# Second layer of an FNet block: the first of seven Strassen products taken in two levels too, in a unit of three

## The chip, the cores and the metric

One core of one Trainium2 chip. The metric is the device time of one execution in microseconds (us). The kernel before takes 1074.35 us, the median of three runs (1073.09 to 1074.63). The engines are called PE (TensorE, matmul), DVE (VectorE), ACT (ScalarE), POOL (GpSimd) and SP (SyncE, which issues most DMA transfers here).

## The reference

Eight batches, 576 tokens, 8 heads of 64, all in fp32. Linear attention is followed by an FNet block with width D = 512 and a two-layer network of 2048 hidden values:

```python
q_s = softmax(q, axis=-1); k_s = softmax(k, axis=2)
kv = einsum('bhsd,bhse->bhde', k_s, v)
x = einsum('bhsd,bhde->bhse', q_s, kv)           # -> (B, S, 512)
mixed = real(fft(fft(x, axis=1), axis=2))
u = x + mixed
un = (u - mean(u)) / sqrt(var(u) + 1e-06)
out = u + maximum(un @ w_ch1, 0.0) @ w_ch2       # 512 -> 2048 -> 512
```

## The kernel before, in words

*Tiling.* The 8 × 576 tokens are nine groups of 512. The first group goes through the two layers with plain matmuls while the weights are prepared. The other eight are called order 1 to order 8 (in code, `order` up to `B` = 8). Each order has an `up` stage (first layer, 512 → 2048) and a `down` stage (second layer, 2048 → 512, added to `u`). Meanwhile the attention and the Fourier mix of the next group are interleaved, so that each order finds its normalised input `unT` ready.

*One level.* A layer is a matrix product A·B cut into 2 × 2 blocks, computed by the Strassen–Winograd scheme with seven products of half size, numbered 1 to 7 and taken in `ORDER` = (1, 6, 5, 7, 2, 4, 3). Each product has its own left side (a sum of blocks of A, slots 0 to 6) and right side (a sum of blocks of B). The left sides of the second layer are the hidden activations, made in `up`: four blocks come out of the first layer, and `a_side` (L383 to L386) makes four sums of blocks of 128 × 512 for each of four pairs j. `A_AT` tells which slot a product reads.

*Two levels.* In orders 2 to 8, `deep_down` computes most of the seven products of the second layer by seven inner products again. Two of them, a unit such as (2, 4), run interleaved: for each inner number n of `ORDER` one inner product of each. An inner product is four matmuls of 128 columns in the source, which the trace holds as eight records on PE; its right side, 128 × 512, is one of the blocks of `w2d` in DRAM. `a_step` (L1317) makes the inner left sides: number 4, 5, 2 and 6 are sums of two 128 × 512 blocks in SBUF. The three PSUM banks `ba`, `bb`, `bc` collect the inner products (`place`), and `ends` empties them: a copy `s1` and the copy `out(0)` on ACT, and on DVE `plus` (L1378): `u2` = bb + s1 after n = 6, `u3` = bb + s1 and `out(3)` after n = 7, `out(2)` after n = 4 and `out(1)` after n = 3, which closes the unit. Product n = 7 adds into the same bank `bb` that `u2` reads. With the unit closed, its two results lie in SBUF, and `into` (L1321, a sum of 128 × 512) adds each to a quarter of the group's output; `sums` (L1324) adds one result to another. Both run on `E`: POOL in orders 2 to 7 and DVE in order 8.

Orders 2 to 7 take product 1 in one level (`single`, L1341: 16 source matmuls of 256 columns, 32 records), then the units (2, 4), (7, 6), (5, 3). Order 8 takes singles 1 and 2, the units (7, 6) and (5, 3), and single 4. Order 1 takes all seven in one level; during it `deepen` (L1279) makes the inner right sides of products 2 to 7, two subtractions on DVE and two on POOL for each, and SP stores the blocks to `w2d` (L1285), 42 blocks of 256 KB.

*Weights.* They stream from DRAM through four slots of 1 MB. `plan` lists the pieces in the order of their use (eight of the first layer an order, then those of the second); when PE has issued the last matmul of piece n, `used` has SP load piece n + 4 into its slot (L454).

*What sets the order.* Each step carries a written-out time, in units of 0.87 us from order 1 on: PE's inner product takes one unit, a stage `up` 56 (`UP`), a stage `down` 50 (`TWICE`) in orders 2 to 8. The steps are sorted by that time and issued, and each engine runs its instructions in this order; it waits by semaphores for what an instruction needs. During `down` the mix of the next group runs: five `block` products (L997, L1000), then two sets of `mix` steps, three in orders 2, 4 and 6. A set of mix steps copies on ACT, computes `eo` from a PSUM bank on DVE (L1042, L1043), and adds it to the rows of `x` (L1054 for 257 columns, L1055 for 255, both SBUF to SBUF on DVE). `norm` for the next group follows at 29 units; in order 7 it is at 14.

Of the kernel before, what the change touches and what calls it, by code (L numbers as in the profile page):

```python
# [78 lines left out]
UNITS = ((2, 4), (7, 6), (5, 3))  # L79
DEEP = [(m, n) for unit in UNITS for n in ORDER for m in unit]  # L80
UP, TWICE = NP * len(ORDER), 8 + 6 * len(ORDER)
# [55 lines left out]
class _Block:  # L137
    def __init__(self, ctx, tc, q, kT, v, w1, w2, ft, cd, out):
# [51 lines left out]
        self.plan, self.base = [], {}  # L190
        for at in range(1, B + 1):
            self.base[at] = len(self.plan)
            self.plan += [self.w1s[p][:].rearrange("p a n -> p (a n)") for pair in PAIRS for p in pair]
            one = lambda m: self.w2s[WB_AT[m]].rearrange("p a n -> p (a n)")
            first = self.first_deep(at)
            self.plan += [one(m) for m in (ORDER if at == 1 else (1, 2) if at == B else (1,))]
            if at > 1:
                for i in range(first, len(DEEP), 4):
                    self.plan.append(self.w2d[:, i:min(i + 4, len(DEEP)), :].rearrange("p a n -> p (a n)"))
            if at == B:  # L200
                self.plan.append(one(4))
# [242 lines left out]
    def first_deep(self, order):  # L444

        return 2 * len(ORDER) * (order == B)

    def load(self, n):

        if n >= len(self.plan):  # L450
            return
        k = (n + 3) % 4
        w = self.big[:, k * NP * HD:(k + 1) * NP * HD]
        self.nc.sync.dma_start(w[:, :self.plan[n].shape[1]], self.plan[n])  # L454
        self.stream[n] = w.rearrange("p (a n) -> p a n", n=HD)
# [776 lines left out]
    def up(self, order, g):  # L1232

        nc, V = self.nc, self.nc.vector
        steps = []
        base, e = self.base[order], V if order == B else nc.gpsimd
        for j in range(NP // 2):
            hp = lambda i, h=self.hpairs(j, 2): h[:, :, i, :]

            def product(m, bank, first, j=j):  # L1240
                def run(i):
                    w = self.stream[base + 2 * j + i]
                    for k in range(2):
                        nc.tensor.matmul(bank()[:, i, :], lhsT=w[:, WA_AT[m], k * P:(k + 1) * P],  # L1244
                                         rhs=self.unT[g][:, B_AT[m], k, :], start=first and i == 0 and k == 0,
                                         stop=k == 1,
                                         skip_group_check=True)
                return [lambda i=i: run(i) for i in range(2)]

            def c11(bank, _, hp=hp):  # L1250
                return [(0, lambda: nc.scalar.activation(hp(0), bank()[:], ACT.Relu))]

            def other(i, hp=hp):
                def run(bank, u):
                    steps = [(0, lambda: V.tensor_tensor(out=hp(i), in0=bank()[:], in1=u()[:], op=ALU.add)),  # L1255
                             (0.8, lambda: nc.scalar.activation(hp(i), hp(i), ACT.Relu))]  # L1256
                    if i == 2:
                        steps.append((1.6, lambda: self.a_side(hp, hp, e, e)))
                    return steps
                return run  # L1260

            job = self.strassen(product, 1, {(1, 1): c11, (2, 1): other(1), (2, 2): other(3), (1, 2): other(2)})
            t = 2 * len(ORDER) * j
            steps += at(t, job) + [(t + 2 * len(ORDER) - 0.5 + 5 * i * (j < NP // 2 - 1), lambda n=base + 2 * j + i: self.used(n)) for i in range(2)]
        return steps
# [25 lines left out]
    def deep_down(self, g, order):  # L1291

        nc, V, G = self.nc, self.nc.vector, self.nc.gpsimd
        base, last, skip = self.base[order] + NP, order == B, self.first_deep(order)
        E = V if last else G
        order = (1, 2, *UNITS[1:], 4) if last else (1, *UNITS)
        h = [self.hpairs(p) for p in range(NP)]
        un = lambda i: self.unT[g][:, i].rearrange("p k n -> p (k n)").rearrange("p (f n) -> p f n", n=P)
        dead = lambda m: lambda i: self.hblock(A_AT[m], *((0, 1), (1, 0), (1, 1))[i])
        temps = {4: lambda i: un(i), 2: lambda i: un(3 + i), 7: self.gap, 6: dead(1), 5: (lambda i: un(i)) if last else dead(4), 3: (lambda i: un(3 + i)) if last else dead(2)}  # L1300
        result = {m: self.hblock(A_AT[m], 0, 0) for m in A_AT}
# [6 lines left out]
        def own(m):  # L1308
            def get(i):
                return temps[m](i - 4) if i > 3 else self.hblock(A_AT[m], i // 2, i % 2)  # L1310
            return get

        def a_step(m, o):
            x, y, e, op = {4: (2, 3, V, ALU.add), 5: (4, 0, V, ALU.subtract), 2: (0, 2, V, ALU.subtract),
                           6: (1, 5, E, ALU.subtract)}[o]
            to = own(m)
            e.tensor_tensor(out=to(o), in0=to(x), in1=to(y), op=op)  # L1317
# [12 lines left out]
        def bank(n, size=P):  # L1330
            box[n] = self.ps.tile([P, 2, size], F32, tag=n, name=n)

        def temp(n):
            box[n] = self.work.tile([P, 2, P], F32, tag=n, name=n, bufs=1)
            return box[n][:]

        def single(m, n, name, i, q):
            if q == 0 and (m != 1 or i == 0):
                bank(name, HD)
            for p in range(4 * q, 4 * q + 4):  # L1340
                nc.tensor.matmul(box[name][:, i, :], lhsT=h[p][:, A_AT[m], i * P:(i + 1) * P],  # L1341
                                 rhs=self.stream[n][:, p, :], start=p == 0 and (m != 1 or i == 0), stop=p == NP - 1,
                                 skip_group_check=True)
            if (i, q) == (1, 1):
                self.used(n)

        def one():
            nc.scalar.copy(tile(1), box["bb"][:].rearrange("p c (e n) -> p c e n", n=P))
# [10 lines left out]

        def product(unit, n, i):  # L1360
            m = unit[i]
            q = DEEP.index((m, n))
            q -= skip
            chunk = base + 1 + last + q // 4
            w = self.stream[chunk]
            first = i == 0 and n in (1, 6, 5)
            if first:
                bank(place[n])
            for f in range(4):
                r = q % 4 * 4 + f  # L1370
                nc.tensor.matmul(box[place[n]][:, i, :], lhsT=own(m)(A_AT[n])[:, f, :],  # L1371
                                 rhs=w[:, r // 2, r % 2 * P:r % 2 * P + P], start=first and f == 0, stop=f == 3,
                                 skip_group_check=True)
            if q % 4 == 3 or q + skip == len(DEEP) - 1:
                self.used(chunk)
# [4 lines left out]
        def ends(unit, n):  # L1380
            first, last = (A_AT[m] for m in unit)
            step = last - first
            out = lambda j: self.hpairs(j)[:, first:last + (1 if step > 0 else -1):step, 0:P]
            if n == 1:
                nc.scalar.copy(temp("s1"), box["ba"][:])
            if n == 6:
                plus(temp("u2"), "bb", "s1")
            if n == 7:
                plus(temp("u3"), "bb", "s1")
# [3 lines left out]
            if n == 4:  # L1393
                plus(out(2), "bb", "s1")
# [3 lines left out]
        after = {(2, 4): [(7, into, 1, 0, 4), (9, into, 0, 0, 2)],  # L1398
# [3 lines left out]
        names = {1: ("bb", "bb"), 2: ("bc", "bb"), 4: ("ba", "bb")}  # L1402
        n, t = 2 * len(ORDER), 0
        for i, unit in enumerate(order):
            if unit in A_AT:
                w = base + (i if i < 2 else 2 + (len(DEEP) - skip) // 4)
                for k in range(4):
                    put(t + 2 * k, single, unit, w, names[unit][k // 2], k // 2, k % 2)
                t += 8
                if unit == 1:  # L1410
                    put(t - 0.5, one)
                    put(t + 1, into, 0, 0, 1)
                    continue
                for c in range(2):
                    put(t - 4.5 + 4 * c, add, names[unit][c], unit // 4, 0, c)
                    if unit == 4 and c == 0:
                        steps.extend(self.scatter(t - 3.7, g, c, 1, lambda: self.xpart(g, 0, 1)))
                    else:
                        half(t - 3.7 + 4 * c, c, unit // 4, 0)
                continue  # L1420
            step = 3 if i < 3 else 2
            early = 6 if last and t < n + 8 else 0 if t == 8 else t - n + 2 if i == 2 else t - n + (0 if last else 3)
            for k, o in enumerate((4, 5, 2, 6)):
                for j, m in enumerate(unit):
                    put(early + step * k + j * 1.1 + 0.3, a_step, m, o)
            for k, o in enumerate(ORDER):
                for j in range(2):
                    put(t + 2 * k + j, product, unit, o, j)
                put(t + 2 * k + 1.5, ends, unit, o)
# [3 lines left out]
        if last:  # L1433
            half(t - 8 + 2, 1, 1, 1)
# [7 lines left out]
    def down(self, g, order):  # L1442
# [5 lines left out]
        for k, m in enumerate(ORDER):  # L1448
            if m != 1:
                spare = [self.hblock(A_AT[ORDER[k - 1]], a, b) for a in range(2) for b in range(2)]  # L1450
                n = self.base[order] + NP + k
                steps += at(t * k - 4 * (k % 2 == 0), self.deepen(m, n, spare if k % 2 else [self.gap(i) for i in range(4)]))

        def product(m, bank, first):
            n = self.base[order] + NP + ORDER.index(m)

            def run(i, q):
                w = self.stream[n]
                for p in range(4 * q, 4 * q + 4):
                    nc.tensor.matmul(bank()[:, i, :], lhsT=h[p][:, A_AT[m], i * P:(i + 1) * P], rhs=w[:, p, :],  # L1460
# [74 lines left out]
def kernel(ctx: ExitStack, tc: tile.TileContext, q, kT, v, w1, w2, ft,  # L1535
# [3 lines left out]
    def timed(t, order, g):  # L1539
# [4 lines left out]
        if b == B:  # L1544
            return steps + at(t + UP + 14, blk.norm(groups[b]))
# [139 lines left out]
```

## Time and profile before

| what | value |
|---|---|
| median of three runs | 1074.35 us (1073.09 to 1074.63) |
| profiled execution, its own time | 1072.76 us |
| span of that execution, mean granted clock | 1071.0 us, 0.999 |
| PE busy | 1058.3 us (99%), 6394 records |
| DVE busy | 685.9 us (64%), 1317 instructions |
| POOL busy | 422.5 us (39%), 352 instructions |
| ACT busy | 404.8 us (38%), 953 instructions |
| DMA | 235.9 MB, mean 220 GB/s; SP's queue busy 63.8% of 16 engines' span |
| `down` of order 2 from / 3 / 4 / 5 | 358.1 / 474.9 / 589.6 / 706.5 us |
| `down` of order 6 / 7 / 8 from | 821.2 / 924.5 / 1021.2 us |
| last matmul, end of the span | 1066.7, 1071.0 us |

The span runs from the first to the last instruction that the profiler recorded; the execution's own time has what lies around it, 1.8 us more. The records of PE's matmuls overlap, so the distance between two starts tells what one costs, not its duration. A line number in a view is that of the code printed above, of the kernel before; the lines of the changed kernel lie 15 to 20 further down.

### The profile page before, as it was taken

To read this page: it belongs to the slowest core of one execution; us is meant where nothing else is said; L and a number is where in the kernel's file an instruction comes from. 1 tells how busy PE (TensorE), PEld (TensorE's weight loads), DVE (VectorE), ACT (ScalarE), POOL (GpSimd) and SP (SyncE) were. 2 spreads that over 40 slices of the span, in tenths; PEclk is the share of its full clock that TensorE was granted. 3 is DMA by queue.
4 is the path that set the end of the run, shared out by engine and by line. 5 is a ranking of instruction groups with operands and counts; after the bars stand their busy time and mean duration, and the time that the engine had idled before them with its cause. 6 is when DMAs were issued, how large, how long until landed. Compare 5 with 4: busy or idle time off the path is not lost.

```text
span 1071.0 us, 16992 instructions
## 1 busy us (share of the span) xinstructions
PE 1058.3 (99%) x6394; PEld 922.4 (86%) x6394; DVE 685.9 (64%) x1317; ACT 404.8 (38%) x953; POOL 422.5 (39%) x352
## 2 busy tenths in 40 slices
PE   8999999999999999999999999999999999999998
PEld 7744556988898899889998999889988998899898
DVE  6897787684455874677556765687457742563563
ACT  5675534632245215521453234522552132131210
POOL 3262220265412743454515543374336353552000
PEclk9999999999999999999999999999999999999999
DMA  9486578648976576646755576547644674576464
GB/s 341 160 302 245 174 246 292 208 162 282 329 262 212 179 252 233 225 177 202 273 178 190 196 246 224 199 183 256 222 167 158 210 257 164 203 249 217 176 214 146
DMA packets 112933, 235.90 MB, mean 220 GB/s; under 512 B 22756, under 2 KB 74212, under 8 KB 102228
## 3 DMA queue, kind: packets, MB, share of 16 engines
q1 hardware_dynamic: 112244, 233.90, 63.8%
q8 instruction: 51, 0.84, 0.3%
q10 hardware_dynamic: 480, 0.52, 0.1%
q0 software_dynamic: 128, 0.39, 0.1%
q14 instruction: 30, 0.25, 0.1%
HBM read 199.66 MB, written 38.93 MB: 223 GB/s over the span
## 4 chain that ended last, share of the span: by engine, by line
PE 84%; DVE 3%; ACT 2%; issue 1%; POOL 1%; DMA 0%; POOLq 0%; DVEq 0%; ACTq 0%
PE bb L1244 15%; PE bb L1371 10%; PE bc L1244 10%; PE ba L1244 10%; PE bc L1371 6%; PE ba L1371 6%; PE bb L1341 4%; PE acc L716 2%; PE acc L884 2%; PE bc L1181 2%; PE bb L1460 2%; PE acc L997 2%; PE acc L1000 2%; PE acc L1025 2%; PE bc L1460 1%; PE ba L1460 1%
## 5 line engine op out<-in xcount | busy, mean ns | idle before, releaser
L1244 PE MATMUL bb<-unT,big 128*128 128x256 f32 x768 | 184.4, 380 | 0.8 <-DVE u L1214 0.8
L1244 PEld LDWEIGHTS bb<-unT,big 128*128 128x128 f32 x768 | 142.5, 190 | 20.3 <-DVE u L1214 2.3
L383 POOL TENSOR_TENSOR big<-big 128x512 f32<-128x512 f32 x28 | 35.9, 1281 | 255.9 <-ACT big L1256 255.9
L1256 ACT ACTIVATE big<-big 128x512 f32<-128x512 f32 x96 | 60.6, 631 | 194.9 <-DVE big L1255 194.5
L1244 PE MATMUL ba<-unT,big 128*128 128x256 f32 x512 | 123.8, 379 | 0.0
L1244 PE MATMUL bc<-unT,big 128*128 128x256 f32 x512 | 123.5, 380 | 0.0
L1214 DVE TENSOR_TENSOR u<-bb,s 128x512 f32<-128x512 f32 x66 | 45.6, 691 | 117.7 <-PE bb L1244 97.4
L1371 PE MATMUL bb<-big 128*128 128x128 f32 x848 | 105.2, 275 | 1.8 <-DVE u L1378 1.8
L1244 PEld LDWEIGHTS bc<-unT,big 128*128 128x128 f32 x512 | 94.7, 190 | 12.5 <-DVE big L1255 1.0
L1244 PEld LDWEIGHTS ba<-unT,big 128*128 128x128 f32 x512 | 94.4, 190 | 12.2 <-issue 0.5
L1371 PEld LDWEIGHTS bb<-big 128*128 128x128 f32 x848 | 99.6, 192 | 2.2 <-DVE u L1378 2.2
L1321 POOL TENSOR_TENSOR x<-x,big 128x512 f32<-128x512 f32 x45 | 57.7, 1297 | 62.7 <-issue 32.9
L1317 DVE TENSOR_TENSOR big<-big 128x512 f32<-128x512 f32 x94 | 78.1, 875 | 2.5 <-POOL big L386 2.5
L1371 PE MATMUL ba<-big 128*128 128x128 f32 x640 | 79.6, 275 | 0.0
L766 ACT ACTIVATE q<-q,qm 128x64 f32<-128x64 f32 x248 | 67.5, 342 | 31.2 <-DVE qm L760 25.9
L1371 PEld LDWEIGHTS ba<-big 128*128 128x128 f32 x640 | 76.3, 192 | 1.2
L1341 PE MATMUL bb<-big 128*128 128x256 f32 x256 | 58.7, 380 | 0.0
L1378 DVE TENSOR_TENSOR u<-bb,s 128x256 f32<-128x256 f32 x40 | 16.8, 421 | 64.6 <-PE bb L1371 59.9
L1255 DVE TENSOR_TENSOR big<-bc,u 128x512 f32<-128x512 f32 x64 | 44.0, 687 | 21.9 <-PE bc L1244 21.0
L1341 PEld LDWEIGHTS bb<-big 128*128 128x128 f32 x256 | 48.2, 190 | 8.0 <-DVE big L1255 1.1
L1371 PE MATMUL bc<-big 128*128 128x128 f32 x416 | 51.5, 275 | 0.0
L1371 PEld LDWEIGHTS bc<-big 128*128 128x128 f32 x416 | 48.9, 192 | 0.0
(265 smaller groups left out, 2014.8 us busy)
## 6 DMA issues: line engine op xcount, KB each, us to landing
big<-w2d SPq DMA_DIRECT2D x67, 1024.0 KB, 4.8
big<-w1s SPq DMA_DIRECT2D x64, 896.0 KB, 4.9
big<-w2s SPq DMA_DIRECT2D x16, 1024.0 KB, 6.4
big<-in_w_dram SPq DMA_DIRECT2D x21, 512.0 KB, 6.3
w2d<-big SPq DMA_DIRECT2D x42, 256.0 KB, 5.6
q<-in_q_dram SPq DMA_DIRECT2D x28, 256.0 KB, 6.4
k<-in_kT_dram SPq DMA_DIRECT2D x24, 288.0 KB, 5.6
v<-in_v_dram SPq DMA_DIRECT2D x24, 256.0 KB, 4.4
```

The lines of the kernel that those rows point to most:

```text
L383: e1.tensor_tensor(out=to(4), in0=at(2), in1=at(3), op=ALU.add)
L716: nc.tensor.matmul(pk, lhsT=ks[:, c, :], rhs=v[:, c, :], start=(c == 0), stop=(c == NC - 1))
L766: nc.scalar.activation(q[:, h, :], q[:, h, :], ACT.Exp, bias=m[:, h:h + 1])
L1214: plus = lambda t: V.tensor_tensor(out=temp(t), in0=box["bb"][:], in1=box["s1"][:], op=ALU.add)
L1244: nc.tensor.matmul(bank()[:, i, :], lhsT=w[:, WA_AT[m], k * P:(k + 1) * P], rhs=self.unT[g][:, B_AT[m], k, :], start=first and i == 0 and ...
L1255: steps = [(0, lambda: V.tensor_tensor(out=hp(i), in0=bank()[:], in1=u()[:], op=ALU.add)), (0.8, lambda: nc.scalar.activation(hp(i), hp(i) ...
L1256: (0.8, lambda: nc.scalar.activation(hp(i), hp(i), ACT.Relu))]
L1317: e.tensor_tensor(out=to(o), in0=to(x), in1=to(y), op=op)
L1321: E.tensor_tensor(out=x, in0=x, in1=tile(m), op=ALU.add)
L1341: nc.tensor.matmul(box[name][:, i, :], lhsT=h[p][:, A_AT[m], i * P:(i + 1) * P], rhs=self.stream[n][:, p, :], start=p == 0 and (m != 1 or ...
L1371: nc.tensor.matmul(box[place[n]][:, i, :], lhsT=own(m)(A_AT[n])[:, f, :], rhs=w[:, r // 2, r % 2 * P:r % 2 * P + P], start=first and f == ...
L1460: nc.tensor.matmul(bank()[:, i, :], lhsT=h[p][:, A_AT[m], i * P:(i + 1) * P], rhs=w[:, p, :], start=first and i == 0 and p == 0, stop=p == ...
```

## The change

Product 1 of the second layer joins the first unit of orders 2 to 7, which becomes (1, 2, 4): three outer products run interleaved, with the inner order (1, 5, 6, 2, 7, 4, 3); the other units keep `ORDER`. In that unit n = 4 gets the bank `ba` and is added to `u3` instead of `bb` and `s1`. A down stage of orders 2 to 8 has 49 units of time instead of 50. Along with it:

- `deepen` also runs for product 1 in order 1, so `w2d` has 49 blocks, and is read by 13 pieces an order (the last of one block) instead of one of `w2s` and eleven.
- Slots 2 and 3 of the left sides change places, so that products 1, 2, 4 lie side by side and one instruction of `ends` empties all three. The `a_step`s write their sums to other dead buffers.
- All `a_step`s of the first unit run on DVE (number 6 ran on POOL). Four more of them are there, for product 1. `into` of product 1 comes 5 units after the unit, ahead of the two at 7 and 9; it came just after the single. The ACT copy `one` is gone.
- In `up`, the `a_side` of the last pair j = 3 runs on DVE instead of POOL, and 4.5 units later (2.8 in order 8).
- Order 7: all sums (`E`, and every `a_side`) on DVE; `norm` for the last group at 26.4 units instead of 14.
- Order 8: singles 1 and 2 become a two-level unit (1, 2), its pieces cut from the same blocks with product 4 left out; single 4 stays.

```diff
-UNITS = ((2, 4), (7, 6), (5, 3))
-DEEP = [(m, n) for unit in UNITS for n in ORDER for m in unit]
-UP, TWICE = NP * len(ORDER), 8 + 6 * len(ORDER)
+UNITS = ((1, 2, 4), (7, 6), (5, 3))
+WITHIN = {1: (1, 5, 6, 2, 7, 4, 3), 7: ORDER, 5: ORDER}
+DEEP = [(m, n) for unit in UNITS for n in WITHIN[unit[0]] for m in unit]
+UP, TWICE = NP * len(ORDER), 7 * len(ORDER)
+SLOT = {0: 0, 1: 1, 2: 3, 3: 2, 4: 4, 5: 5, 6: 6}
+H_AT = {m: SLOT[i] for m, i in A_AT.items()}
...
-        base, e = self.base[order], V if order == B else nc.gpsimd
+        base, e = self.base[order], V if order >= B - 1 else nc.gpsimd
+        wait = {1: 0, B: 2.8}.get(order, 4.5)
...
-                        steps.append((1.6, lambda: self.a_side(hp, hp, e, e)))
+                        steps.append((1.6 + wait * (j == NP // 2 - 1), lambda e=V if order > 1 and j == NP // 2 - 1 else e: self.a_side(hp, hp, e, e)))
...
-        E = V if last else G
-        order = (1, 2, *UNITS[1:], 4) if last else (1, *UNITS)
+        E = V if order >= B - 1 else G
+        order = ((1, 2), *UNITS[1:], 4) if last else UNITS
...
-        temps = {4: lambda i: un(i), 2: lambda i: un(3 + i), 7: self.gap, 6: dead(1), 5: (lambda i: un(i)) if last else dead(4), 3: (lambda i: un(3 + i)) if last else dead(2)}
+        temps = {1: self.gap, 2: un, 4: lambda i: un(3 + i), 7: lambda i: self.gap((0, 1, 3)[i]), 6: lambda i: un((0, 1, 6)[i]),
+                 5: (lambda i: un(3 + i)) if last else dead(4), 3: dead(2)}
...
-                           6: (1, 5, E, ALU.subtract)}[o]
+                           6: (1, 5, V if m in UNITS[0] else E, ALU.subtract)}[o]
...
+        def bank_of(unit, n):
+            return "ba" if n == 4 and unit[0] == 1 else place[n]
...
-                plus(out(2), "bb", "s1")
+                plus(out(2), *(("ba", "u3") if unit[0] == 1 else ("bb", "s1")))
...
-        after = {(2, 4): [(7, into, 1, 0, 4), (9, into, 0, 0, 2)],
+        after = {(1, 2, 4): [(5, into, 0, 0, 1), (7, into, 1, 0, 4), (9, into, 0, 0, 2)], (1, 2): [(4, into, 0, 0, 1), (5, into, 0, 0, 2)],
...
-                if unit == 1:
-                    put(t - 0.5, one)
-                    put(t + 1, into, 0, 0, 1)
-                    continue
...
+            size = len(unit)
+            n = size * len(ORDER)
+            if i == 0:
+                starts = (0.2, 2.5, 8.5 if size == 3 else 5.5, 11.5 if size == 3 else 7)
+            else:
+                early, step = (max(t - 11, 7), 3) if i == 1 else (t - 11 - 3 * last, 2)
+                starts = [early + step * k + 0.3 for k in range(4)]
+            for at_o, o in zip(starts, (4, 5, 2, 6)):
                 for j, m in enumerate(unit):
-                    put(early + step * k + j * 1.1 + 0.3, a_step, m, o)
-            for k, o in enumerate(ORDER):
-                for j in range(2):
-                    put(t + 2 * k + j, product, unit, o, j)
-                put(t + 2 * k + 1.5, ends, unit, o)
+                    put(at_o + j * (1.1 if i else 0.75), a_step, m, o)
+            for k, o in enumerate(WITHIN[UNITS[i][0]]):
+                for j in range(size):
+                    put(t + size * k + j, product, unit, o, j)
+                put(t + size * k + size - 0.5, ends, unit, o)
...
-            return steps + at(t + UP + 14, blk.norm(groups[b]))
+            return steps + at(t + UP + 26.4, blk.norm(groups[b]))
```

## The prediction

> **What bounds the kernel now.** First the shares of busy time and the chain of waits. The first line below gives busy time per engine; the second is the chain that ended last, by engine.
>
> ```profile
> PE 1058.3 (99%) x6394; PEld 922.4 (86%) x6394; DVE 685.9 (64%) x1317; ACT 404.8 (38%) x953; POOL 422.5 (39%) x352
> ...
> PE 84%; DVE 3%; ACT 2%; issue 1%; POOL 1%; DMA 0%; POOLq 0%; DVEq 0%; ACTq 0%
> ```
>
> TensorE (PE) sets the time, at a granted clock of 0.999. Its matmul records overlap, so their busy time says little; I use the distance from one start to the next. Summed over the trace, distances beyond the normal come to only some 11 us, most of it in the opening. So a matmul less is time gained, and a wait of PE is time lost in full.
>
> Second, the groups by line, for what the change touches: output and inputs, shape, count, then busy us and mean ns, then idle time before and its releaser.
>
> ```profile
> L1371 PE MATMUL bb<-big 128*128 128x128 f32 x848 | 105.2, 275 | 1.8 <-DVE u L1378 1.8
> ...
> L1341 PE MATMUL bb<-big 128*128 128x256 f32 x256 | 58.7, 380 | 0.0
> ...
> L1317 DVE TENSOR_TENSOR big<-big 128x512 f32<-128x512 f32 x94 | 78.1, 875 | 2.5 <-POOL big L386 2.5
> ```
>
> PE waits within the two-level units for one thing only: the sum `u` that DVE makes (L1378). And L1317, sums of the same size, averages 875 ns where an undisturbed one takes 0.68 us: something holds it up.
>
> Third, the timeline around the end of the first unit of order 4, where PE next depends on DVE (start, duration, engine, line; x2 is two in a row):
>
> ```profile
> 617.48 0.42 DVE L1378 TENSOR_TENSOR big<-bc,u 128x256 f32<-128x256 f32 x1 [0.69 <-PE bc L1371]
> 617.83 0.42 DVE L1054 TENSOR_TENSOR x<-x,eo 128x257 f32<-128x257 f32 x1
> 618.16 1.49 DVE L1055 TENSOR_TENSOR x<-x,eo 128x255 f32<-128x255 f32 x1
> 619.57 0.74 DVE L1042 TENSOR_TENSOR eo<-acc,sn 128x256 f32<-128x256 f32 x2
> ...
> 621.32 0.68 DVE L1317 TENSOR_TENSOR big<-big 128x512 f32<-128x512 f32 x1
> 621.92 0.41 DVE L1378 TENSOR_TENSOR u<-bb,s 128x256 f32<-128x256 f32 x1
> ...
> 618.04 2.74 POOL L1321 TENSOR_TENSOR x<-x,big 128x512 f32<-128x512 f32 x2 [8.79 <-issue]
> ...
> 617.28 1.95 PE L1371 MATMUL ba<-big 128*128 128x128 f32 x16
> ...
> 622.64 1.95 PE L1371 MATMUL bb<-big 128*128 128x128 f32 x16
> ```
>
> The reader is to see three things. The L1055 of half a row takes 1.49 us, against 0.42 for its twin L1054: it began 0.12 us after POOL's first `into` (L1321) and ended 0.24 us after that `into`, at half of 2.74. The sum `u` ends at 622.33. And PE's product n=7, at 622.64, adds into the bank that this `u` reads, so it may not start before: the margin is 0.31 us. PE reaches it 5.36 us after the unit's end at 617.28.
>
> [...] 1.49 against 0.42 us above, and L1042, which reads PSUM, ran at 0.37 us each beside POOL. [...] here two POOL operations in 2.74 us hold exactly two DVE operations, so I use 1.37 us each. [...] These records show 111.7 and 215.5 ns start to start[...].
>
> **The change, part by part.** *Products.* A single is 32 records of 256 columns: 32 × 0.2155 = 6.90 us, which the chain of waits shows in order 8 (second line):
>
> ```profile
> 376.45 1.79 PE bb L1371 x16
> ...
> 1021.16 6.91 PE bb L1341 x32
> ```
>
> A two-level product is 7 × 8 = 56 records of 128, 56 × 0.1117 = 6.25 us (the first line: two products' 16 records in 1.79). So 0.65 us is gained by product 1 in each of orders 2 to 7, and twice in order 8: 8 × 0.65 = 5.2 us.
>
> *Order 1.* Two more subtractions on DVE, two on POOL, and 7 more stores of 256 KB. DVE's next need has 1 us or more of room. On SP a store goes out about each 1 us, so 7 us; the loads behind them leave SP 8 to 11 us apart and their data are used 15 us later. Nothing; if the stores did delay a load beyond that, up to 2 us.
>
> *Loads.* 21 instead of 20 an order, of which one has 256 KB; order 8 has 20 for 18. A 1 MB load lands in 4.8 us, it is issued 10.7 us ahead, and PE uses up a chunk in 4 × 0.894 = 3.57 us. Nothing; queue 1 is at 63.8%.
>
> *DVE within the first unit.* It gains four `a_step`s, two that POOL made, and the last pair's `a_side` (four operations): 10 × 0.60 us = 6 us. In the stretch of this unit DVE was busy 20.3 of 26.5 us (third engine column; POOL 13.2), including blocked time:
>
> ```profile
> 475.00:501.50 26.50, 26.50 (x195) 25.12 (x195) 20.32 (x37) 5.73 (x22) 13.23 (x10) 1.00 0.60 204
> ```
>
> POOL loses six operations there, each of which held one DVE operation about 1 us longer. So DVE's total stays near the same. The steps have 0.7 us or more to their product: nothing, with an upper bound in rival three. The ACT copy of product 1 goes, hidden anyway.
>
> *Behind the first unit.* Here is the loss. `into` of product 1 moves from the single's end to 5 time units after the unit, ahead of the two at 7 and 9. All three wait for the unit's last sum, L1378 `out(1)`, and then run back to back on POOL, while DVE's written order puts four adds of L1054/1055 behind that same sum. Call E the unit's end on PE. `out(1)` is now 384 wide: between 0.42 and 0.69 us, taken as 0.55. It starts at E + 0.2 and ends at E + 0.75. The first add goes free; the next three each meet one `into`, which end at about E + 2.2, 3.5 and 4.9; so the adds end near E + 2.5, 3.9 and 5.2. In orders 3 and 5 an `a_step` (0.6) follows, and `u` ends at E + 6.1 to 6.2, against 5.36 at PE: a stall of 0.8. In orders 2, 4 and 6, which have three sets of mix adds, two L1042, an L1043 and two more adds stand in between, 1.5 us more after the overlap: `u` ends at E + 7.6 to 7.7, a stall of 2.3. The second sum, `u3`, follows `u2` at 3.82 us (505.49 to 509.31 in order 3) where PE needs 3.57: another 0.25.
>
> *Orders 7 and 8.* In order 7 all of POOL's sums move to DVE and the norm moves behind the first unit. Before, DVE's steps were blocked by POOL and PE stood still 1.75 us at 938.51:
>
> ```profile
> 932.44 5.68 DVE L1317 TENSOR_TENSOR big<-big 128x512 f32<-128x512 f32 x4 [2.50 <-POOL big L386]
> ...
> 933.58 3.39 POOL L1317 TENSOR_TENSOR unT<-big,unT 128x512 f32<-128x512 f32 x2
> ```
>
> Four steps take 5.68 us there instead of 2.4. With POOL quiet this stall goes (−1.75); 0.3 comes back in two small waits for sums. DVE, busy 30.9 of the stage's 48.0 us before, has room. Order 8 uses DVE for everything already; the sum `u3` of (7,6) comes about 0.2 late.
>
> *Sum*, in us:
> - orders 2 and 4: −0.65 + 2.31 + 0.25 = +1.9 each
> - orders 3 and 5: −0.65 + 0.81 + 0.23 = +0.4 each
> - order 6: −0.65 + 2.31 + 0.2 − 0.41 (a wait of PE at the same `u` today) = +1.45
> - order 7: −0.65 − 1.75 + 0.3 = −2.1
> - order 8: −1.3 + 0.2 = −1.1
>
> Together 3.8 + 0.8 + 1.45 − 3.2 = +2.85. The profiled execution took 1072.76 with a span of 1071.0, so it becomes 1075.6 with 1073.9. It stands 1.6 us under the median shown, 1074.35; on that the forecast is 1077.2.
>
> **Rivals.** *The `into`s don't hold the adds* (POOL starts later, or the adds run ahead of it): no stall behind the unit, gains −5.2 − 1.75 − 0.41, +0.3 to 0.5 back: −7, 1067.3, faster. For it: SBUF lines on DVE often pass at 0.42. Against: 1.49 at 618.16, just this pair.
>
> *Half of the blocking*: POOL is late enough for two of three to be felt, or the sum `u` gets by earlier: the stalls shrink to 0 (orders 3, 5) and 1 us (2, 4, 6): −7 + 3.3, about −3.5 to 0, so 1071 to 1074.5, near no change. A measurement here tells 0.2%, 2.15 us.
>
> *DVE is full within the first unit*, slower by more: if POOL's remaining `a_side`s and folds hold as many DVE operations as before, the 6 us of added work meet 6.2 us of idle time, spread unevenly. Then steps are late at PE by 1 to 2 us in each of five orders from the point where more than 0.7 us of delay gathers: +5 to +10, on top of the forecast 1082 to 1087.
>
> *The change doesn't do what it says*: if the 128-wide records of the new product ran at 0.123 us, the gain would be gone (56 × 0.123 = 6.90) and the time 1082. All such records show 0.1117, so this gets nearly nothing.
>
> **How the numbers follow.** The forecast as worked out 0.5, with a range of its own of 1074.5 to 1080 (the stall of 2.3 taken between 1.3 and 3.2); no blocking 0.13; half 0.17; DVE full 0.18; something of loads or stores 0.02. The range for 8 in 10 reaches from the lower part of "half" to the near end of "DVE full": 1070 to 1083. Faster by 0.2% is below 1072.2: 0.13 and a part of "half", 0.18. Within, 1072.2 to 1076.5: the rest of "half" and the lower third of the forecast, 0.24. Slower: 0.58.
>
> **What would show it.** Right: groups of L1360 fall to 32 records, and 128-wide ones stay at 0.1117; three POOL L1340 in a row just behind each first unit, with L1071/1072 beside them at 1.2 to 1.5 us; PE's waits for L1397 `u` grow from 1.8 to about 10 us in all, longest in orders 2, 4 and 6; order 7's stage falls from 48.0 to 46 us. Wrong: those adds at 0.42 us; PE waits at L1336 steps inside the first unit; a wait for `w2d` loads; a_sides that start late in order 1.

## The result and the profile after

The changed kernel takes 1082.08 us (median of 4 runs, 1081.28 to 1082.63) against 1074.12 us for the kernel before. The ratio is 1.0075, with a 95% interval of 1.0057 to 1.0092: 8.0 us slower, where 2.85 us were forecast. The profiled execution took 1081.28 us, with a span of 1079.4 us against 1071.0.

The page of the changed kernel, busy time per engine, then the groups that answer to those shown before:

```profile
PE 1059.0 (98%) x6586; PEld 929.2 (86%) x6586; DVE 725.6 (67%) x1418; ACT 402.6 (37%) x948; POOL 340.1 (32%) x291
...
L1390 PE MATMUL bb<-big 128*128 128x128 f32 x824 | 106.3, 282 | 8.6 <-DVE u L1397 8.5
...
L1336 DVE TENSOR_TENSOR big<-big 128x512 f32<-128x512 f32 x114 | 80.6, 733 | 0.0
```

The inner products' wait for `u` has grown from 1.8 to 8.5 us. The `a_step`s on DVE, held less often now, went from 875 to 733 ns. They make nobody wait: the first unit itself runs without a gap on PE in all five orders.

The waits of PE in the changed kernel (total, times, longest, all in us) show that this is the one large wait that came:

```profile
PE bb L1390 <- DVE u L1397: 8.5, 5, 2.3
PE ba L257 <- POOL kvr L159: 2.3, 1, 2.3
PE acc L1014 <- issue: 1.7, 1, 1.7
PE tr L554 <- ACT big L549: 1.4, 2, 0.7
```

This view counts a wait from the modelled end of the record before. Counted from start to start, as the prediction does, the pauses are 0.16 us longer: 2.48 us in orders 2, 4 and 6, and 0.95 us in 3 and 5. The text below gives them in this way.

Now the timeline of the place that the prediction spoke of, behind the first unit of order 4: DVE, then POOL, then PE.

```profile
620.92 0.56 DVE L1397 TENSOR_TENSOR big<-bc,u 128x384 f32<-128x384 f32 x1 [1.17 <-PE bc L1390]
621.39 0.42 DVE L1071 TENSOR_TENSOR x<-x,eo 128x257 f32<-128x257 f32 x1
621.73 1.49 DVE L1072 TENSOR_TENSOR x<-x,eo 128x255 f32<-128x255 f32 x1
623.14 1.49 DVE L1071 TENSOR_TENSOR x<-x,eo 128x257 f32<-128x257 f32 x1
624.55 1.49 DVE L1072 TENSOR_TENSOR x<-x,eo 128x255 f32<-128x255 f32 x1
625.97 0.74 DVE L1059 TENSOR_TENSOR eo<-acc,sn 128x256 f32<-128x256 f32 x2
...
627.49 0.69 DVE L1336 TENSOR_TENSOR big<-big 128x512 f32<-128x512 f32 x1
628.09 0.42 DVE L1397 TENSOR_TENSOR u<-bb,s 128x256 f32<-128x256 f32 x1
...
621.61 4.15 POOL L1340 TENSOR_TENSOR x<-x,big 128x512 f32<-128x512 f32 x3 [8.32 <-issue]
...
628.56 3.67 PE L1390 MATMUL bb<-big 128*128 128x128 f32 x16 [2.32 <-DVE u L1397]
632.02 2.00 PE L1390 MATMUL ba<-big 128*128 128x128 f32 x16
```

The reader sees the first add free at 0.42 us, three held at 1.49 us each by three `into`s in 4.15 us, and `u` at 628.51, 7.8 us behind the unit's end at 620.7. So far it is the prediction's working. The new thing is in the line of 628.56: two inner products, 16 records, start 3.46 us ahead of the next group, at 632.02, where 1.79 is normal. In windows of the same trace (us, PE busy and records, granted clock of PE, DMA share, GB/s):

```profile
624.00:628.00 4.00, 2.24 (x21) 1.00 0.81 270
628.50:632.20 3.70, 3.64 (x18) 0.54 0.21 31
632.20:636.00 3.80, 3.80 (x37) 1.00 0.72 265
```

Behind the pause PE ran at half clock for 3.41 us (628.72 to 632.13): 18 records in 3.7 us, against 37 in 3.8.

The `down` stages, from one's first matmul to the next stage's (order 8: to the last matmul's start), in us:

| order | before | after | difference | forecast | after, profiled again |
|---|---|---|---|---|---|
| 2 | 55.13 | 57.13 | +2.00 | +1.9 | 58.52 |
| 3 | 53.92 | 54.49 | +0.57 | +0.4 | 54.48 |
| 4 | 55.12 | 58.52 | +3.40 | +1.9 | 58.52 |
| 5 | 53.92 | 54.49 | +0.57 | +0.4 | 54.49 |
| 6 | 55.01 | 57.98 | +2.97 | +1.45 | 57.97 |
| 7 | 48.02 | 45.96 | −2.06 | −2.1 | 45.95 |
| 8 | 45.52 | 44.67 | −0.85 | −1.1 | 44.67 |

Together that is +6.6 us of the 8.4 by which the span grew. Of the rest, 1.6 us lie ahead of everything that the change touches: the first matmul of order 1 came at 178.88 us instead of 177.26. The experiments below return to both surprises, the half clock and the opening.

### The profile page after: what moved, and what is told of

Read it like the earlier page. It is cut to its first block, busy times and chain, and to the rows that moved or that the text cites. A ratio compares the mean times of both kernels' runs of the same rounds, so it can differ in the third digit from the quotient of the medians.

```text
span 1079.4 us, 17394 instructions
## 1 busy us (share of the span) xinstructions
PE 1059.0 (98%) x6586; PEld 929.2 (86%) x6586; DVE 725.6 (67%) x1418; ACT 402.6 (37%) x948; POOL 340.1 (32%) x291
## 4 chain that ended last, share of the span: by engine, by line
PE 81%; DVE 6%; ACT 1%; issue 1%; DMA 0%; POOLq 0%; DVEq 0%; ACTq 0%
PE bb L1262 15%; PE bc L1262 10%; PE ba L1262 10%; PE bb L1390 9%; PE ba L1390 8%; PE bc L1390 7%; PE acc L733 2%; PE acc L901 2%; PE bc L1198 2%; PE bb L1480 2%; PE acc L1014 2%; PE acc L1017 2%; PE acc L1042 1%; PE bc L1480 1%; PE ba L1480 1%; PE ba L1198 1%
## 5 line engine op out<-in xcount | busy, mean ns | idle before, releaser
L1390 PE MATMUL ba<-big 128*128 128x128 f32 x928 | 114.1, 275 | 0.0
L1390 PEld LDWEIGHTS ba<-big 128*128 128x128 f32 x928 | 110.3, 192 | 1.5
L1390 PEld LDWEIGHTS bb<-big 128*128 128x128 f32 x824 | 99.9, 197 | 10.5 <-DVE u L1397 10.2
L399 POOL TENSOR_TENSOR big<-big 128x512 f32<-128x512 f32 x19 | 24.2, 1273 | 213.2 <-ACT big L1274 191.4
L1336 DVE TENSOR_TENSOR big<-big 128x512 f32<-128x512 f32 x114 | 80.6, 733 | 0.0
L1340 POOL TENSOR_TENSOR x<-x,big 128x512 f32<-128x512 f32 x45 | 58.5, 1318 | 40.8 <-issue 31.0
L1137 POOL TENSOR_TENSOR unT<-unT 128x512 f32<-128x512 f32 x8 | 14.2, 1769 | 141.5 <-DVE unT L1137 141.5
L1336 POOL TENSOR_TENSOR big<-big 128x512 f32<-128x512 f32 x15 | 24.7, 1663 | 98.0 <-DVE big L1336 88.8
L1390 PE MATMUL bc<-big 128*128 128x128 f32 x432 | 55.4, 275 | 0.0
L1397 DVE TENSOR_TENSOR u<-bb,s 128x256 f32<-128x256 f32 (+1 forms) x42 | 19.3, 459 | 52.6 <-PE bb L1390 44.1
L1390 PEld LDWEIGHTS bc<-big 128*128 128x128 f32 x432 | 52.0, 192 | 0.6
```

Of the source, the lines that this page charges most:

```text
L399: e1.tensor_tensor(out=to(4), in0=at(2), in1=at(3), op=ALU.add)
L1340: E.tensor_tensor(out=x, in0=x, in1=tile(m), op=ALU.add)
L1390: nc.tensor.matmul(box[name][:, i, :], lhsT=own(m)(A_AT[n])[:, f, :], rhs=w[:, r // 2, r % 2 * P:r % 2 * P + P], start=first and f == 0, s ...
```

## The experiments

The theory: POOL's three `into`s hold DVE's adds, which stand ahead of `u2` in DVE's order. Rivals: DVE's order alone is the cause; POOL alone is; DVE is full in the first unit. After the result came a second question: what brings the half clock.

**The three sums on DVE** (`into_dve`).

```diff
-            E.tensor_tensor(out=x, in0=x, in1=tile(m), op=ALU.add)
+            (V if m in UNITS[0] else E).tensor_tensor(out=x, in0=x, in1=tile(m), op=ALU.add)
```

> The changed kernel, but the three `into` sums of the first unit run on DVE in orders 2 to 6, with the same written times, so that POOL has nothing to do behind the unit. Theory (POOL's three `into` sums hold DVE's adds, and so the sum u2): PE's stalls at the first u2 behind the unit, 2.48 us in orders 2, 4, 6 and 0.95 in 3 and 5, go to nothing, and with them the half clock of about 1.4 us behind two of them; the second sum u3, with two `into` sums more ahead of it on DVE, comes 0.2 to 0.5 late. Stage `down` of order 2: 57.1 to about 54.5 us, of order 4: 58.5 to 54.5, of order 3: 54.5 to 53.5. The profiled execution goes from 1081.3 to about 1070 to 1071. Rival (it is the place of the adds in DVE's written order, behind out(1) and ahead of u2, whatever POOL does): stalls of 2 us or more stay in orders 2, 4, 6, and 1.8 us of DVE work comes on top: 1081 to 1084.

Measured: 1069.41 us, ratio to the kernel before 0.9964 (0.9955 to 0.9972). Stages of orders 2 and 4 fell to 54.31 us, as expected, with no wait at `u2` anywhere. Orders 3 and 5 rose to 54.76, because `u3` is now 1.46 us late; expected were 0.2 to 0.5. DVE's timeline in order 3 of this run:

```profile
503.92 0.68 DVE L1340 TENSOR_TENSOR x<-x,big 128x512 f32<-128x512 f32 x1
504.52 1.28 DVE L1336 TENSOR_TENSOR big<-big 128x512 f32<-128x512 f32 x2
505.73 1.76 DVE L1340 TENSOR_TENSOR x<-x,big 128x512 f32<-128x512 f32 x1
507.40 1.75 DVE L1336 TENSOR_TENSOR big<-big 128x512 f32<-128x512 f32 x1
509.08 0.41 DVE L1397 TENSOR_TENSOR u<-bb,s 128x256 f32<-128x256 f32 x1
```

Two `into`s (L1340) stand ahead of `u3` there, and two operations, beside POOL's two `a_step`s, still take 1.76 and 1.75 us instead of 0.68. The rival "DVE's order alone" falls: the adds stand where they stood.

**One `into` of the three later** (`into1_late`), the number of POOL's operations varied alone.

```diff
-(1, 2, 4): [(5, into, 0, 0, 1), (7, into, 1, 0, 4), ...
+(1, 2, 4): [(14.2 if E is G else 5, into, 0, 0, 1), (7, into, 1, 0, 4), ...
```

> The changed kernel, but in orders 2 to 6 the `into` of product 1 alone is moved behind the next unit's sum, so that two `into` sums run on POOL behind the first unit instead of three. Theory: each `into` holds DVE by about 1.1 us, so the stalls of 2.48 us in orders 2, 4, 6 shrink to about 1.4, those of 0.95 in 3 and 5 to nothing, and the half clock behind the long ones stays away: about 1073 to 1074 us. Rival (place of the adds): stalls and time unchanged, 1081.

Measured: 1070.83 us (one run). The stalls in orders 2, 4 and 6 are 1.41, 1.40 and 1.41 us, in orders 3 and 5 only 0.12; there is no half clock. One `into` less makes `u` 2.48 − 1.41 = 1.07 us earlier; that is what each one costs DVE here. The time is 2 to 3 us below the 1073 to 1074 expected, because these numbers were made from the profiled execution with the long opening; in this run the opening was 2.1 us shorter.

**All three later** (`intos_late`).

```diff
-(1, 2, 4): [(5, into, 0, 0, 1), (7, into, 1, 0, 4), (9, into, 0, 0, 2)]
+(1, 2, 4): [(t, into, *x) for t, x in zip((11.5, 13, 14.5) if E is G else (5, 7, 9),
+                                          ((0, 0, 1), (1, 0, 4), (0, 0, 2)))]
```

> The changed kernel, but in orders 2 to 6 all three `into` sums of the first unit stay on POOL and are written 11.5, 13 and 14.5 units behind the unit instead of 5, 7 and 9, behind POOL's own two a_steps. Theory: the five stalls and the half clock go, 12 us; what the later `into` sums hold up on DVE then has slack, or comes back as a wait for u3 or for an a_step of the third unit, up to 1 us an order: 1069 to 1074 us. Rival (place of the adds): unchanged, 1081.

Measured: 1065.79 us, ratio 0.9936 (0.992 to 0.9953). This version beats both kernels. Orders 2 to 6 have no wait left; stages of 54.31, 53.19, 54.31, 53.19 and 53.76 us. Its DVE in order 4, the same instructions as in the fence above:

```profile
615.07 0.42 DVE L1071 TENSOR_TENSOR x<-x,eo 128x257 f32<-128x257 f32 x1
615.40 0.42 DVE L1072 TENSOR_TENSOR x<-x,eo 128x255 f32<-128x255 f32 x1
615.73 0.42 DVE L1071 TENSOR_TENSOR x<-x,eo 128x257 f32<-128x257 f32 x1
616.07 0.42 DVE L1072 TENSOR_TENSOR x<-x,eo 128x255 f32<-128x255 f32 x1
```

Four adds in 1.33 us from start to start of what follows, instead of 4.58. The `into`s run later, from 623.53 us on in order 4, beside sums from PSUM (L1397) and the norm's statistics (L1092), which keep their lengths of 0.4 and 0.7 us.

**The adds earlier, POOL as in the change** (`mix_early`).

```diff
-            steps += at(t + 12.5 + 3.2 * i, some)
+            steps += at(t + 11.2 + 3.2 * i, some)
```

> The changed kernel with all `into` sums where the change put them, but the mix steps of orders 1 to 6 (their matmuls, copies and adds) 1.3 units earlier, so that two of the adds that stood behind the unit's last sum out(1) on DVE now stand ahead of it. Theory (adds and `into` sums together make the stall): in orders 3 and 5 one add and the a_step are held instead of three adds, u2 ends near E + 4.3 us, no stall; in orders 2, 4, 6 two adds are held, u2 near E + 6.4, stall about 1.0 us instead of 2.48. Stages `down` of order 2 about 55.6, of 3 about 53.4 us. Rival (the stall comes from POOL's `into` sums alone, whatever DVE has in its queue): stalls unchanged.

Measured: 1072.13 us (one run), stages of orders 2 and 3 of 55.61 and 53.48 us, stalls 0.96 in orders 2 and 4, 0.19 in 3, as expected; in order 6 it is 1.64 us where 1.0 was expected. The trace shows why: two more adds, 0.33 us each from start to start, which stood behind `u2` there in the change, now stand ahead of it. The rival "POOL alone" falls too. Here it took both: SBUF-to-SBUF sums on POOL, and such sums on DVE, 1.49 us each instead of 0.42, ahead of what PE waits for.

**Order 7's engines alone, in the kernel before** (`order7_alone`).

```diff
-        E = V if last else G
+        E = V if base >= self.base[B - 1] else G
...
-base, e = self.base[order], V if order == B else nc.gpsimd
+base, e = self.base[order], V if order >= B - 1 else nc.gpsimd
```

> The kernel before with one part of the change: in order 7 every `a_side` and the sums `into`, number 6 and `sums` on DVE instead of POOL; norm stays where it was, product 1 stays single. Theory (POOL's sums held DVE's a_steps, and PE waited 1.75 us for them): that stall goes, the stage `down` of order 7 falls from 48.0 to 46.3 us, the span from 1071.0 to about 1069.3. Rival (the norm's later place, not the engine, freed it): the stall stays, 48.0.

Measured: stage 46.17 us (46.3 expected), 1070.08 us in all. DVE's steps ran at their free length, and the stall of 1.75 us was gone:

```profile
932.18 0.69 DVE L1317 TENSOR_TENSOR unT<-big,unT 128x512 f32<-128x512 f32 x1
932.78 0.69 DVE L1317 TENSOR_TENSOR big<-big 128x512 f32<-128x512 f32 x1
933.39 0.69 DVE L1317 TENSOR_TENSOR unT<-big,unT 128x512 f32<-128x512 f32 x1
933.99 0.69 DVE L1317 TENSOR_TENSOR big<-big 128x512 f32<-128x512 f32 x1
```

The gain in order 7 comes from the engine, not from the norm's place. It doesn't need the two-level product.

**The last `a_side` back on POOL** (`aside_pool`).

```diff
-lambda e=V if order > 1 and j == NP // 2 - 1 else e: self.a_side(hp, hp, e, e)
+lambda e=e: self.a_side(hp, hp, e, e)
```

> The changed kernel with the `a_side` of the last pair back on POOL in orders 2 to 6, at the changed time. It prices that edit and the third rival of the prediction. If POOL's four sums hold DVE's first a_steps (four operations, 1.1 us each, against margins of about 0.7 us): PE waits 1 to 2 us within the first unit in each of five orders, stages 2 to 6 that much longer, 1086 to 1091 us. If the a_steps have room: stages unchanged within 0.2 us.

Measured: 1102.52 us (one run), far beyond what was expected. PE waits once in the first unit of each of five orders:

```profile
PE bc L1390 <- DVE unT L1336: 12.4, 5, 2.5
PE bb L1390 <- DVE u L1397: 8.5, 5, 2.3
```

In order 2 DVE and POOL of this run read:

```profile
362.37 1.36 DVE L981 TENSOR_TENSOR eo<-eo 128x128 f32<-128x128 f32 x1
363.76 1.31 DVE L982 TENSOR_TENSOR eo<-eo 128x128 f32<-128x128 f32 x1
364.99 1.35 DVE L981 TENSOR_TENSOR eo<-eo 128x128 f32<-128x128 f32 x1
366.37 1.30 DVE L982 TENSOR_TENSOR eo<-eo 128x128 f32<-128x128 f32 x1
367.60 0.68 DVE L1336 TENSOR_TENSOR unT<-big 128x512 f32<-128x512 f32 x1
...
361.99 1.59 POOL L399 TENSOR_TENSOR big<-big 128x512 f32<-128x512 f32 x1 [2.02 <-ACT big L1274]
363.65 1.26 POOL L400 TENSOR_TENSOR big<-big 128x512 f32<-128x512 f32 x1
```

Four column folds of the mix (L981, L982), 0.28 us each when free, are held at 1.3 us by the four `a_side` sums, and the `a_step` behind them comes some 4 us later than it would. The folds work on `eo` and the sums on `big`, so it isn't a dependence between their data that holds them. The pause of 2.64 us brought half clock as well: order 2's stage took 62.77 us. So the move of this `a_side` to DVE, which the prediction took as neutral for DVE, is worth at least 2.64 us of pause an order; without it the third rival would have come true, by more than its +5 to +10 us.

**Number 6 of the first unit back on POOL** (`a6_pool`).

```diff
-6: (1, 5, V if m in UNITS[0] else E, ALU.subtract)
+6: (1, 5, E, ALU.subtract)
```

> The changed kernel with the a_steps of number 6 of the first unit (three of them) on POOL in orders 2 to 6, where they stood before, at the changed times. Prices that edit. If DVE has room in the first unit, as the trace of the changed kernel says (no wait of PE there): three DVE operations held by about 1.1 us each, 1.8 us of DVE work gone, the inner product that reads number 6 is the last of the unit: stages within 0.3 us of the changed kernel. If DVE is at its limit there: 1 us or more longer in each of five stages.

Measured: every stage as in the changed kernel to within 0.03 us, apart from order 2, where the half clock came (58.51). That edit is worth nothing either way.

**The half clock: pauses of chosen length** (`pauses_a` and `pauses_b`), on the version with the late `into`s. Only the repeats of `u2` in the unit (7, 6) are added:

```diff
                 plus(temp("u2", len(unit)), "bb", "s1")
+                for _ in range(extra if unit == (7, 6) else 0):
+                    plus(box["u2"][:], "bb", "s1")
```

> The kernel with the three `into` sums late (no stall behind the first unit), in which DVE now computes the sum u2 of the unit (7, 6) again 8, 10, 10, 12, 13 times in orders 2 to 6, each 0.335 us, the same values into the same place. PE's pause there is that less the slack of 0.8 us (orders 2, 4, 6) or 1.1 us (3, 5): about 1.9, 2.2, 2.5, 2.9, 3.5 us. Theory (the half clock seen in orders 4 and 6 of the changed kernel follows a PE pause from about 2.4 us on, in any order): half clock, 3.5 us long and worth about 1.4 to 1.7 us, behind the last three pauses, none behind the first; the second is open. Rival (it belongs to orders 4 and 6, not to the pause): behind orders 4 and 6 alone, not 5.

> As the run before, with the repeats the other way round: 13, 12, 10, 10, 8 in orders 2 to 6, pauses of about 3.6, 2.9, 2.5, 2.2, 1.9 us. Theory: half clock in orders 2, 3 and 4, none in 6. Rival: in orders 4 and 6 again.

Each repeat took about 0.45 us and not 0.335 (nine in 4.08 us), so the pauses were longer than planned: 2.92, 3.53, 3.84, 4.45 and 5.22 us in the first run, 5.22, 4.45, 3.84, 3.53 and 2.93 us in the second. Half clock came behind all but the first of these ten, order 2 of `pauses_a`. The rival that ties it to orders 4 and 6 falls. Behind the 2.93 us of the second run PE first ran 1.2 us at full clock and then fell, in windows of order 6:

```profile
880.70:881.90 1.20, 1.20 (x10) 1.00 0.00 0
881.90:885.30 3.40, 3.40 (x18) 0.50 0.72 231
```

**The changed kernel once more** (`after_again`), nothing altered.

> The changed kernel, not altered, profiled once more. Theory (the half clock behind a pause of 2.48 us comes or stays away by chance, and so does the length of the opening): the pauses of 2.48 and 0.95 us come again to within 0.1 us, the half clock of about 1.4 us behind a varying number of the three long ones, the opening between 176.5 and 179 us. Rival (both are the change's own): half clock again behind orders 4 and 6 and not 2, opening again 178.9.

Measured: 1080.44 us. The pauses are 2.48, 0.95, 2.48, 0.95 and 2.48 us again, the half clock came behind all three long ones, and order 1 began at 176.69 us. So the 178.88 of the first profile is no part of the change. Some of it is half rate too: at the start of the kernel, matmuls of 128 columns started 213 ns apart up to 14.29 us in the first profile (17 records from 10.66 us on), and up to 11.63 us in the kernel before (6 from 10.35 us on).

Counting all profiled runs from order 1 on, by the length of PE's pause: from 0.9 to 1.75 us, half clock behind 0 of 17; from 2.47 to 2.93 us, behind 16 of 19; from 3.5 to 5.2 us, behind 8 of 8.

What tells the 16 of the 19 from the other 3 is where the pause fell. In every run, the recorded clock of PE changed only at times that lie whole multiples of 3.413 us apart, to within 2 ns; in the first profile of the changed kernel these times are 628.72, 632.13, 864.24, 867.65 and 1079.28 us. Call the stretches of 3.413 us clock windows. Cut into them, the first profile of the changed kernel reads as follows (columns as in the windows above). The first two lines are order 2, whose pause is split over both clock windows, 1.28 and 1.20 us; the third is order 4, whose pause lies within one, and the fourth is what came behind it.

```profile
389.79:393.20 3.41, 2.29 (x21) 1.00 0.80 279
393.20:396.61 3.41, 2.21 (x19) 1.00 0.22 53
625.31:628.72 3.41, 1.09 (x10) 1.00 0.64 269
628.72:632.13 3.41, 3.41 (x17) 0.50 0.23 34
```

Of the 44 pauses counted above, the 24 with half clock behind them put 1.96 us or more into one clock window, and the clock was half from that window's end on. The 20 without put no more than 1.75 us into any. One of these is the pause of 2.92 us in `pauses_a`, which fell as 1.31 and 1.62 us; the 2.93 us of `pauses_b` fell as 0.73 and 2.19 us and brought half clock. This was read from the traces afterwards: no run placed its pauses in the clock windows on purpose. Nor are the cases of one run independent: in `after_again` the half clock began at 393.12, 628.64 and 864.16 us, 69 clock windows apart each time.

## Why the prediction was right or wrong

*Bound and place: right.* PE stays the bound, and the one new wait is the one named: `u2` behind the first unit, longest in orders 2, 4 and 6.

*The stalls: right, a little short.* Forecast were 2.3 and 0.8 us, measured 2.48 and 0.95. `out(1)` 384 wide took 0.56 us (0.55 was taken), three adds 1.49 each. `u3` 0.24 us later: as forecast.

*The sum: wrong by a missing term.* "A wait of PE is time lost in full" counted a pause at its own length. It cost more: behind 24 of the 27 pauses of 2.47 us and more PE ran at half clock, for 3.41 us or twice that. The stages of order 2 with and without it differ by 58.52 − 57.13 = 1.39 us, since a part goes into the wait for `u3` that otherwise follows. With that term for two or three orders, 2.8 to 4.2 us, the under-sized stalls (3 × 0.17 + 2 × 0.14 = 0.8) and order 8's 0.25, the forecast of +2.85 becomes +6.7 to +8.1; the stages gave +6.6 in one profile and +8.0 in the other, the medians +8.0. The least of a pause that half clock followed was 1.96 us within one clock window; pauses of 2.48 us brought it in 10 of 12 cases here. The prediction had no term for what follows a pause.

*The products: right.* In the version without stalls order 2 gains 0.82 us: 0.65 for the product, and two waits of 0.08 us that the kernel before had there.

*Order 7: right* (−2.06 against −2.1), and shown by the run of that part alone. *Order 8:* −0.85 against −1.1; `u3` is late by 0.23 us where about 0.2 was forecast, and two more gaps of 0.1 us came with it.

*Order 1 and the loads: right.* Order 1's stage is 57.23 us before and after, with seven stores more. No wait for a `w2d` load appears.

*DVE in the first unit: right for the change as made,* no wait there. But it rests on the `a_side` moved to DVE, which the prediction took as neutral; the run without that move shows what it protects from.

*The rivals.* "No blocking" fell in the trace, and so did "half". "DVE full" did not happen. The time lay inside the range of 1070 to 1083, near its upper end, but beyond the 1074.5 to 1080 that the worked-out case allowed itself. The upper part of the range had been put there for a full DVE, and the half clock filled it: that was luck.

## What to carry to other kernels

When a step moves to another time, list what runs beside it on both DVE and POOL: here a POOL sum on SBUF operands cost 1.07 us of the critical path where a short DVE sum from SBUF stood ahead of what PE needed (`into1_late`), and nothing where it ran beside DVE's sums from PSUM, which kept their 0.4 us, or where nobody waited (`intos_late`). Three steps written later turned a loss of 8.0 us into a gain of about 7 (ratio 0.9936). And a pause of PE of about 2.5 us or more should be priced with the half clock, which followed 24 of 27 such pauses here and cost about 1.4 us of a stage.

## What the runs showed of the hardware

- Half clock came behind pauses of 2.47 to 2.93 us in 16 of 19 cases, of 3.5 us and more in 8 of 8, of up to 1.75 us in none of 17. Between 1.75 and 2.47 us nothing was measured. The matmuls of 128 columns started 213 ns apart instead of 112, the first of them 0.3 to 1.5 us after the pause.
- The granted clock changed only at times whole multiples of 3.413 us apart within a run. It fell to half at the end of a clock window that held 1.96 us or more of a pause (24 of 24), and not where none held more than 1.75 us (20 of 20). It stayed half for two windows where the pause reached 0.73 us or more into the first of these (6 cases), and for one where it reached 0.24 us or less (18 cases).
- DVE sums of 256 columns repeated from PSUM into the same tile started 0.46 us apart (`pauses_a`, nine in 4.08 us). In the kernel before, a sum that reads the `u` made just ahead of it started 0.46 us behind (495.25 and 495.71 us), and an operation that reads nothing of its forerunner 0.33 us behind such a sum (500.05 and 500.38 us).
